# A spectral layer and a mixture of experts on one core: biases moved from TensorE to VectorE, the inverse spread over the steps

## The chip, the cores and the metric

The kernel runs on one core of a Trainium2 chip. The metric is the device time of the program in microseconds (us). TensorE is PE in the profile, its weight loads PEld, VectorE DVE, ScalarE ACT, GpSimd POOL, and SyncE, which issues most transfers, SP.

## The reference

```python
X = np.fft.rfft(x, axis=1)                 # x: 8 x 2496 x 256
Yr = Xr @ w_r - Xi @ w_i + b_r
Yi = Xr @ w_i + Xi @ w_r + b_i
Yr = np.sign(Yr) * np.maximum(np.abs(Yr) - 0.01, 0.0)      # Yi the same
y = np.fft.irfft(Yr + 1j * Yi, n=2496, axis=1)
# mixture of experts over the 19968 rows of y, 8 experts, the best one each:
out[mask] = gate_w[mask] * (np.maximum(y[mask] @ w1[e], 0) @ w2[e])
```

## The kernel before

The transform of length 2496 = 39 x 64 is done as two matrix products with a trip through DRAM between them. `fwd_a` (L280) does the 39-point part for two groups of a batch: a product pa into a PSUM bank of the tag "u", copied to ae and written to the spectrum in DRAM; eleven of them make a batch. `turn` (L295) reads the spectrum back transposed, as t. A **step** is one of ten slices of a batch, 80 in all, and step it = 10 b + s is slice s of batch b.

In a step, `fwd_b` (L302) does the 64-point part of the next step's slice as pb, and `halves` (L313) splits it into a rounded part sh and a rest sl, because the products with the weights are done as three products of rounded halves: ACT reads pb into re and sh, DVE makes the sum su and sl, then ACT and DVE make the third slot of sh and sl from su. `mix` (L328) multiplies: pk is the product with w_r of the sum, copied by ACT to k; pm holds the two others, and DVE adds k to both, giving the tile v (u in the code). The biases are added on PE: each half of pm begins with a product of a tile of ones and a tile that holds the bias in two rows (L335, `split_bias`, L252). `shrink` (L355) is the soft threshold of the step before: ACT makes r, DVE four pieces of y. `inv_b` (L371) multiplies y of an earlier step back to 64 points (pv, tag "u"), and ACT copies it into z, which holds a whole batch.

`inv_a` (L384) is the last part: of twelve **pieces** of a batch, each does two groups of pz from z (tag "u", one product that also gives the gate's logits), split by ACT and DVE into zh and zl, and the py of the piece before (tag "yo"), copied by ACT to yb. z has one copy, so the pieces of batch b-1 are all done in steps 2 to 5 of batch b, three a step ("turning"), and the pv of those steps wait till step 6, two a step, held as y in six buffers.

After eleven groups `route` (L581) is queued as a job: 23 small DVE operations, an exponential (ex, L594) on ACT and two small products, cut into pieces that `tick` emits one by one. They give each token its expert, its gate and its slot; `scatter` writes the rows to the experts' lists in DRAM by indirect transfers on POOL, `send` one by one, held back by `pace`. `table` gives the experts' tiles of 256 tokens. The last batch's pieces are interleaved with the first seven tiles (`finish_last`, L551), and 82 tiles are done in all (`up`, L885, and `down`, L914).

The order of every engine but POOL is the order of the code. PSUM has eight banks: four of tag "u" (pa, pv, pz, and po of the first tiles), two of "yo" (py, pk and the routing's), one for pb, one for pm.

Of the kernel before, what the change touches and what calls it, by code (L numbers as in the profile page):

```python
# [100 lines left out]
class Kernel:  # L101
    def __init__(self, tc, nb, x, w_r, w_i, b_r, b_i, w_gate, w1, w2,
# [6 lines left out]
        assert (nb - 3) * S - E * (TT - 1) > (EARLY - 1) * TT  # L109
# [27 lines left out]
    def open_inverse(self, st, pst):  # L137
# [35 lines left out]
        self.z = k.tile([128, 2, 66, 40], F32, name="z")  # L173

    def open_forward(self, st):
# [3 lines left out]
        self.xp = self.pool(self.xst, "xp", 5)  # L179
# [9 lines left out]
        self.bias = f.tile([128, 2, D], F32R, name="bias")  # L189
        self.ones = f.tile([128, 128], F32R, name="ones")  # L190
# [6 lines left out]
        self.braw = self.w.tile([33, 2, D], F32, tag="y", name="braw", bufs=6)  # L197
        for h, b in ((0, self.b_r), (1, self.b_i)):
            for q in (0, 32):
                nc.gpsimd.dma_start(self.braw[q:q + 1, h, :], b.rearrange("(o n) -> o n", o=1))  # L200
# [11 lines left out]
        nc.gpsimd.memset(self.z[:, :, 64:66, :], 0.0)  # L212
# [39 lines left out]
    def split_bias(self):  # L252
        nc = self.nc
        zero = self.w.tile([128, 2, D], F32, tag="y", name="zero", bufs=6)
        nc.vector.memset(zero, 0.0)
        nc.vector.tensor_copy(self.bias, zero)
        nc.vector.tensor_scalar_add(self.ones, zero[:, 0, 0:128], 1.0)
        bh = self.w.tile([33, 2, D], F32R, tag="y", name="bh", bufs=6)
        nc.scalar.copy(self.bias[0:1], self.braw[0:1])
        nc.scalar.copy(bh[32:33], self.braw[32:33])  # L260
        nc.vector.tensor_sub(self.bias[32:33], self.braw[32:33], bh[32:33])

# [65 lines left out]
    def mix(self, b, s):  # L328
# [3 lines left out]
        def product(nm, slot, to):  # L332
            i = 0 if nm == "r" else 1
            if i:
                nc.tensor.matmul(to, self.ones, self.bias[:, 1 if nm == "d" else 0, :], start=True, stop=False)  # L335
            for c in range(2):
                for a, ww in ((sh, self.wh), (sh, self.wl), (sl, self.wh)):
                    nc.tensor.matmul(to, a[:, c, slot, :], ww[nm][:, c, :], start=i == 0, stop=i == (5 if nm == "r" else 6))
# [13 lines left out]
        nc.vector.tensor_add(u, p, k.unsqueeze(1).broadcast_to((128, 2, D)))  # L352
        self.us[b, s] = u

    def shrink(self, b, s):  # L355
# [5 lines left out]
        y = self.w.tile([128, 2, D], F32, tag="y", name="y", bufs=6)  # L361
# [9 lines left out]
    def inv_b(self, b, s):  # L371
        nc = self.nc
        y = self.ys.pop((b, s))
        p = self.psi.tile([128, 512], F32, tag="u", name="pv", bufs=4).rearrange(
            "p (c a r n) -> p c a r n", c=2, a=2, r=2)
        for kp in range(2):
            for c in range(2):
                nc.tensor.matmul(p[:, c, kp, :, :], y[:, kp, c * 128:(c + 1) * 128], self.bi[:, 2 * s + kp, :],  # L378
                                 start=True, stop=True)
        for c in range(2):  # L380
            nc.scalar.copy(self.z[:, c, 0:NB, 4 * s:4 * s + 4].rearrange("p n a -> p a n"),  # L381
                           p[:, c].rearrange("p a r n -> p (a r) n"))

    def inv_a(self, b, i):  # L384
        nc = self.nc
        for g in (2 * i, 2 * i + 1) if i < GH else ():
            p = self.psi.tile([128, 512], F32, tag="u", name="pz", bufs=4)
            for c in range(2):
                nc.tensor.matmul(p[:120, c * 136:(c + 1) * 136],  # L389
                                 self.z[:, c, 3 * g:3 * g + 3, :].rearrange("p j a -> p (j a)"), self.iw[:, c, :],  # L390
# [6 lines left out]
        for g in (2 * i - 2, 2 * i - 1) if i else ():  # L397
# [10 lines left out]
    def spectral(self, fwd):  # L408
# [14 lines left out]
        self.split_bias()  # L423
        self.turn(0, 0)
        self.turn(0, 1)
# [28 lines left out]
        for it in range(n):  # L454
# [16 lines left out]
            if turning:  # L471
                inverse()
# [538 lines left out]
```

## Time and profile before

| | |
|---|---|
| median of 3 runs | 1549.95 us (1549.72 to 1550.38) |
| the profiled execution: time, span | 1556.04 us, 1554.3 us |
| mean granted TensorE clock | 0.992 of full speed |
| DVE, ACT, POOL busy | 59%, 50%, 25% of the span |
| HBM read, written | 241.99 MB, 66.37 MB |

The spectral part runs to about 582 us, and the rest is the last batch's pieces and the tiles. A timeline row gives start, duration and the instruction, with the number of instructions merged in the row; a duration reaches to the end of the last write, so the next instruction of an engine may start before it. The length of a repeated step is therefore read from start to start.

### The profile page before, as it was taken

The numbers are of one execution on the slowest core, as the hardware profiler recorded it, in microseconds if no ns is written. First come the engines' busy times: TensorE is split into PE (matmuls) and PEld (weight loads), VectorE is DVE, ScalarE is ACT, GpSimd is POOL, SyncE is SP. The second block draws the span as 40 slices with busy tenths as digits, with TensorE's granted clock in tenths as the row PEclk, the third lists the DMA queues.
The fourth block names the chain that finished last, engine by engine and source line by source line (L and its number), as shares of the span: only waits on it lengthen the run. The fifth ranks groups of instructions, "written<-read, shape, count | busy, mean of one in ns | idle before, by whom it ended". The sixth has DMA issues, their size and how long they took to land. (4 is left out here: it accounts for less than half of the span.)

```text
span 1554.3 us, 35598 instructions
## 1 busy us (share of the span) xinstructions
PE 1516.7 (98%) x10934; PEld 1398.6 (90%) x10934; DVE 912.2 (59%) x2102; ACT 782.2 (50%) x1689; POOL 394.8 (25%) x554
## 2 busy tenths in 40 slices
PE   6999999999999999999999999999999999999997
PEld 3899999998989888889999999999999999999996
DVE  3677787777778777655455545545445445445442
ACT  2667777777767666344344434434334334334332
POOL 1002433425151534334311111111112111111111
PEclk7999999999999999999999999999999999999998
DMA  8864554646353422334234332323213213132210
GB/s 238 231 193 115 174 145 136 179 119 195 111 172 94 147 58 61 84 91 121 65 100 106 95 77 72 97 52 94 56 42 98 49 47 103 42 78 69 49 42 21
DMA packets 192834, 159.94 MB, mean 103 GB/s; under 512 B 127770, under 2 KB 163264, under 8 KB 192365
## 3 DMA queue, kind: packets, MB, share of 16 engines
q1 hardware_dynamic: 172685, 113.43, 28.8%
q0 software_dynamic: 19936, 44.04, 8.5%
q8 instruction: 89, 1.46, 0.4%
q14 instruction: 124, 1.02, 0.2%
HBM read 241.99 MB, written 66.37 MB: 198 GB/s over the span
## 5 line engine op out<-in xcount | busy, mean ns | idle before, releaser
L939 PE MATMUL po<-h,hh 128*128 128x512 f32 x1312 | 462.1, 395 | 0.0
L902 PE MATMUL ph<-xh,h 128*128 128x256 f32 x1312 | 372.0, 284 | 1.8 <-DVE hl L908 1.8
L902 PE MATMUL ph<-xl,h 128*128 128x256 f32 x1312 | 371.1, 283 | 0.0
L902 PE MATMUL ph<-xh,l 128*128 128x256 f32 x1312 | 370.7, 283 | 0.0
L936 PE MATMUL po<-h,hl 128*128 128x256 f32 x1148 | 324.0, 282 | 0.2 <-DVE hl L908 0.2
L908 DVE SCALAR_TENSOR_TENSOR hl<-ph,hh 128x512 fp32r<-128x512 f32 x328 | 226.2, 690 | 149.3 <-ACT hh L907 114.2
L907 ACT ACTIVATE hh<-ph 128x512 fp32r<-128x512 f32 x328 | 193.8, 597 | 204.0 <-PE ph L902 198.4
L939 PEld LDWEIGHTS po<-h,hh 128*128 128x128 f32 x1312 | 241.5, 188 | 43.8 <-issue 0.2
L948 POOL DMA_INDIRECT out<-o,row x124 | 123.8, 998 | 581.1 <-DVE o L946 472.7
L902 PEld LDWEIGHTS ph<-xh,l 128*128 128x128 f32 x1312 | 251.0, 191 | 3.7
L902 PEld LDWEIGHTS ph<-xh,h 128*128 128x128 f32 x1312 | 251.0, 191 | 3.2 <-DVE hl L908 3.2
L946 DVE SCALAR_TENSOR_TENSOR o<-po,xr,part 128x256 f32<-128x256 f32 x156 | 75.4, 484 | 302.6 <-ACTq L864 153.7
L902 PEld LDWEIGHTS ph<-xl,h 128*128 128x128 f32 x1312 | 251.1, 191 | 0.0
L945 ACT ACTIVATE part<-po,xr 128x256 f32<-128x256 f32 x156 | 73.8, 473 | 334.1 <-PE po L939 324.9
L936 PEld LDWEIGHTS po<-h,hl 128*128 128x128 f32 x1148 | 215.6, 188 | 6.3 <-DVE hl L908 2.1
L644 POOL DMA_INDIRECT xs_dram<-yb,pos x176 | 176.7, 1004 | 74.4 <-issue 63.8
L365 DVE SCALAR_TENSOR_TENSOR y<-v,r 64x256 f32<-64x256 f32 x320 | 134.0, 419 | 6.9 <-ACT r L359 0.8
L389 PE MATMUL pz<-iw,z 128*120 128x136 f32 x704 | 96.9, 280 | 2.5 <-DVE zl L395 1.7
L308 PE MATMUL pb<-bm,t 128*128 128x128 f32 x640 | 86.8, 279 | 12.3 <-DMA t<-spec_dram 9.5
L381 ACT COPY z<-pv 128x256 f32<-128x256 f32 x160 | 94.3, 712 | 5.9 <-PE pv L378 2.9
L308 PEld LDWEIGHTS pb<-bm,t 128*128 128x128 f32 x640 | 80.0, 195 | 13.5 <-issue 11.2
L389 PEld LDWEIGHTS pz<-iw,z 128*120 128x120 f32 x704 | 87.7, 183 | 3.5 <-DVE zl L395 1.9
(181 smaller groups left out, 2557.7 us busy)
## 6 DMA issues: line engine op xcount, KB each, us to landing
r<-moe_w SPq DMA_DIRECT2D x672, 128.0 KB
r<-moe_w SPq DMA_DIRECT2D x166, 512.0 KB
xq<-xs_dram SPq DMA_DIRECT2D x332, 64.0 KB
spec_dram<-ae SPq DMA_DIRECT2D x88, 240.0 KB
t<-spec_dram SPq DMA_DIRECT2D x160, 128.0 KB
x<-x SPq DMA_DIRECT2D x40, 384.0 KB
x<-x SPq DMA_DIRECT2D x40, 84.0 KB
xs_dram<-yb,pos POOLq DMA_INDIRECT x176
```

The costliest lines, as they stand in the source:

```text
L308: nc.tensor.matmul(p[:, c, :, kp, :], t[:, kp, c * 128:(c + 1) * 128], self.bm[:, 2 * s + kp, :], start=True, stop=True)
L365: nc.vector.scalar_tensor_tensor(out=y[q * 64:q * 64 + 64, kp, :], in0=u[h, q, :], scalar=LAM, in1=r[h, q, :], op0=ALU.add, op1=ALU.min)
L381: nc.scalar.copy(self.z[:, c, 0:NB, 4 * s:4 * s + 4].rearrange("p n a -> p a n"), p[:, c].rearrange("p a r n -> p (a r) n"))
L389: nc.tensor.matmul(p[:120, c * 136:(c + 1) * 136], self.z[:, c, 3 * g:3 * g + 3, :].rearrange("p j a -> p (j a)"), self.iw[:, c, :], start ...
L644: i = nc.gpsimd.indirect_dma_start(out=self.xs[:, :], out_offset=bass.IndirectOffsetOnAxis(ap=pos[:n, g:g + 1], axis=0), in_=y[:n, g, 0:XW ...
L902: nc.tensor.matmul(p[:, i, :], a[:, c, f * 128:(f + 1) * 128], v[:, c, :], start=m == 0, stop=m == 5)
L907: nc.scalar.activation(hh[:, s, :], p, AF.Relu)
L908: nc.vector.scalar_tensor_tensor(out=hl[:, s, :], in0=p, scalar=0.0, in1=hh[:, s, :], op0=ALU.max, op1=ALU.subtract)
L936: nc.tensor.matmul(p[:, :D], hl[:, f - 1, hs], w2[:, f - 1, 0, :], start=False, stop=False)
L939: nc.tensor.matmul(p, hh[:, f, hs], w2[:, f].rearrange("p a d -> p (a d)"), start=f == 0, stop=f == 7)
L946: nc.vector.scalar_tensor_tensor(out=o[:, h, :], in0=p[:, :D], scalar=xr[:, h, 0:1], in1=part, op0=ALU.mult, op1=ALU.add)
L948: i = nc.gpsimd.indirect_dma_start(out=self.out[:, :], out_offset=bass.IndirectOffsetOnAxis(ap=at[h], axis=0), in_=o[:, h, :], in_offset=N ...
```

## The change

z gets a second copy, used by even and odd batches in turn. The twelve pieces of a batch are spread over steps 2 to 11 behind the batch's own ten, one or two a step, and each pv is done two steps behind its mix. The two bias matmuls of each step go: the biases are loaded to all partitions by two transfers (the old row tiles, tile of ones and `split_bias` go), and k becomes a DVE operation that adds both biases to pk and writes twice the width. pk gets a bank of its own, and tag "u" has three banks. The first routing pieces of a step stand between v and su. The last two pieces of batch 6 stand behind the last step, where eight filler products stood. There are four x tiles in place of five, five ae in place of eight, three y in place of six; the first table is made from step 56 on in place of 61, and a step sends two or three scattered groups of rows in place of three.

```diff
-        assert (nb - 3) * S - E * (TT - 1) > (EARLY - 1) * TT
+        assert (nb - 4) * S - E * (TT - 1) > (EARLY - 1) * TT
...
-        self.z = k.tile([128, 2, 66, 40], F32, name="z")
+        self.zs = [k.tile([128, 2, 66, 40], F32, name=f"z{i}") for i in range(2)]
...
-        self.xp = self.pool(self.xst, "xp", 5)
+        self.xp = self.pool(self.xst, "xp", 4)
...
-        self.bias = f.tile([128, 2, D], F32R, name="bias")
-        self.ones = f.tile([128, 128], F32R, name="ones")
+        self.bias = f.tile([128, 2, D], F32, name="bias")
...
-        p = self.psi.tile([128, 512], F32, tag="u", name="pa", bufs=4)
+        p = self.psi.tile([128, 512], F32, tag="u", name="pa", bufs=3)
...
-        ae = self.xp.tile([120, 2, D], F32, tag="ae", name="ae", bufs=8)
+        ae = self.xp.tile([120, 2, D], F32, tag="ae", name="ae", bufs=5)
...
         def product(nm, slot, to):
-            i = 0 if nm == "r" else 1
-            if i:
-                nc.tensor.matmul(to, self.ones, self.bias[:, 1 if nm == "d" else 0, :], start=True, stop=False)
+            i = 0
...
-        pk = self.psi.tile([128, 512], F32, tag="yo", name="pk")
+        pk = self.psi.tile([128, 512], F32, tag="k", name="pk", bufs=1)
         product("r", 2, pk[:, :D])
-        k = self.w.tile([128, D], F32, tag="k", name="k", bufs=2)
-        nc.scalar.copy(k, pk[:, :D])
-        self.pace(k[0:1, 0:1])
+        k = self.w.tile([128, 2, D], F32, tag="k", name="k", bufs=2)
+        nc.vector.tensor_add(k, pk[:, :D].unsqueeze(1).broadcast_to((128, 2, D)), self.bias)
+        self.pace(k[0:1, 0, 0:1])
...
-        nc.vector.tensor_add(u, p, k.unsqueeze(1).broadcast_to((128, 2, D)))
+        nc.vector.tensor_add(u, p, k)
...
-        y = self.w.tile([128, 2, D], F32, tag="y", name="y", bufs=6)
+        y = self.w.tile([128, 2, D], F32, tag="y", name="y", bufs=3)
...
     def inv_a(self, b, i):
+        self.inv_z(b, i)
+        self.inv_y(b, i - 1)
...
-        self.split_bias()
         self.turn(0, 0)
         self.turn(0, 1)
+        for h, v in ((0, self.b_r), (1, self.b_i)):
+            self.nc.sync.dma_start(self.bias[:, h, :], bass.AP(v.tensor, v.offset, [[0, 128], [1, D]]))
...
         for b in range(nb):
             for s in range(10):
-                o = s + 2 if b == 0 or s > 7 else 6 + s // 2
-                if 10 * b + o < n:
-                    back[10 * b + o].append((b, s))
+                if 10 * b + s + 2 < n:
+                    back[10 * b + s + 2] = (b, s)
+        pieces = {i: [] for i in range(n)}
+        for b in range(nb - 1):
+            for i, o in enumerate((2, 3, 3, 4, 5, 5, 6, 7, 8) if b == nb - 2 else (2, 3, 4, 4, 5, 6, 7, 8, 8, 9, 10, 11)):
+                pieces[10 * b + 10 + o].append((b, i))
...
+            self.tick(3 if it < n - 10 else 4)
             if it + 1 < n:
                 self.fwd_b(*todo[it + 1])
                 half = self.halves(*todo[it + 1])
                 next(half)
...
             mix = self.mix(b, s)
+            next(mix)
+            for _ in itertools.chain(small, half):
+                pass
...
             for a in first[it]:
                 self.fwd_a(*a)
+            if back[it]:
+                for _ in self.inv_b(*back[it]):
+                    pass
             self.tick(1)
+            self.nudge()
+            for a in pieces[it][:1]:
+                self.inv_a(*a)
             next(mix, None)
+            self.tick(3 if it >= n - 5 else 1)
+            self.nudge()
+            if s % 2 or b >= nb - 2:
+                self.pace(self.us[b, s][0:1, 0, 0:1])
+                self.send(1)
+            for a in pieces[it][1:]:
+                self.inv_a(*a)
...
-            if b == nb - 2 and s == 1:
+            if b == nb - 3 and s == 6:
                 self.tabling = self.table(0)
...
-        self.keep_warm(8)
-        self.inv_b(*todo[n - 1])
+        self.inv_z(nb - 2, 9)
+        self.inv_y(nb - 2, 8)
+        self.inv_z(nb - 2, 10)
+        self.tick(3)
+        for _ in self.inv_b(*todo[n - 1]):
+            pass
+        self.inv_y(nb - 2, 9)
+        self.inv_y(nb - 2, 10)
...
     def breathe(self):
-        self.tick(3)
-        self.nudge()
+        self.tick(4)
...
-                self.psi.tile([128, 512], F32, tag="u", name="po", bufs=4)
+                self.psi.tile([128, 512], F32, tag="k" if h else "u", name="po", bufs=1 if h else 3)
```

The places where the order matters, as the engines' programs have it (a row is a line of the kernel, the instruction, what it writes and reads; xN: so many alike).

PE, from the last product of pk on; before, in a step with two pv:

```order
L338 MATMUL pk<-whr,sl 128x256
L284 MATMUL pa<-x,far 120x512
L378 MATMUL pv<-bi,y 128x128 x4
L335 MATMUL pm<-bias,ones 128x256
L338 MATMUL pm<-whd,sh 128x256
L338 MATMUL pm<-wld,sh 128x256
```

The same place of the change, in a step with one piece:

```order
L321 MATMUL pk<-whr,sl 128x256
L269 MATMUL pa<-x,far 120x512
L361 MATMUL pv<-bi,y 128x128 x4
L377 MATMUL pz<-iw,z_107 120x136 x4
L394 MATMUL py<-zh,gh 117x272
L394 MATMUL py<-zh,gl 117x272
L394 MATMUL py<-zl,gh 117x272
```

The bias product is gone, pv stands behind pa, and pz and py of a piece stand between them and pm.

ACT, a step with an exponential of a routing job; before:

```order
L319 COPY re<-pb 128x256
L320 CAST sh<-pb 128x2x256
L359 ACTIVATE r<-v,nlam 128x512
L324 CAST sh<-su 128x2x128
L594 ACTIVATE ex<-lg 117x88
L381 COPY z<-pv 128x4x64 x2
L344 COPY k<-pk 128x256
L292 COPY ae<-pa 120x512
```

and of the change, from the eviction of py on:

```order
L395 COPY yb<-py 117x272 x2
L585 ACTIVATE ex<-lg 117x88
L304 COPY re<-pb 128x256
L305 CAST sh<-pb 128x2x256
L342 ACTIVATE r<-v,nlam 128x512
L309 CAST sh<-su 128x2x128
L277 COPY ae<-pa 120x512
L365 COPY z_108<-pv 128x4x64 x2
```

ex stood behind re, sh, r and sh, and stands ahead of them now.

DVE, around su, with the last operations of a routing job; before:

```order
L352 TENSOR_TENSOR v<-pm,k 128x512
L321 TENSOR_TENSOR su<-re,pb 128x256
L322 TENSOR_TENSOR sl<-pb,sh 128x2x256
L325 TENSOR_TENSOR sl<-su,sh 128x2x128
L626 TENSOR_TENSOR carry<-carry,scan_102 117x8
L628 CAST carry_b<-carry 117x8
L630 SCALAR_TENSOR_TENSOR rb<-pr,base 117x8
L365 SCALAR_TENSOR_TENSOR y<-v,r 64x256 x2
L633 TENSOR_TENSOR lg<-scan_102,rb 117x88
```

and of the change:

```order
L335 TENSOR_TENSOR v<-pm,k 128x512
L617 TENSOR_TENSOR carry<-carry,scan_102 117x8
L619 CAST carry_b<-carry 117x8
L621 SCALAR_TENSOR_TENSOR rb<-pr,base 117x8
L624 TENSOR_TENSOR lg<-scan_102,rb 117x88
L625 TENSOR_TENSOR lg<-lg,scan_100 117x88
L306 TENSOR_TENSOR su<-re,pb 128x256
L307 TENSOR_TENSOR sl<-pb,sh 128x2x256
L327 TENSOR_TENSOR k<-pk,bias 128x512
L348 SCALAR_TENSOR_TENSOR y<-v,r 64x256 x4
```

The five routing operations stood behind su and sl and among the pieces of y, and stand between v and su now; the new k stands between sl and y.

## Rows read from the trace of the kernel before

**Rows 1.** The page of the profiled execution: its span, and busy time by engine.
```profile
span 1554.3 us, 35598 instructions
...
PE 1516.7 (98%) x10934; PEld 1398.6 (90%) x10934; DVE 912.2 (59%) x2102; ACT 782.2 (50%) x1689; POOL 394.8 (25%) x554
```

**Rows 2.** Stretches A:B in us: length, busy time by engine (instructions), clock, DMA share, GB/s.
```profile
99.81:450.39 350.58, 349.79 (x2703) 322.41 (x2702) 265.67 (x740) 258.41 (x635) 125.40 (x209) 1.00 0.51 147
450.39:494.42 44.03, 41.89 (x326) 38.79 (x324) 33.75 (x116) 29.89 (x79) 10.02 (x16) 1.00 0.34 99
494.42:576.74 82.32, 78.93 (x652) 76.05 (x651) 66.89 (x191) 56.38 (x139) 35.25 (x57) 1.00 0.41 113
```

**Rows 3.** PE in order of time, step 9 (start us, us, instruction).
```profile
78.87 1.05 PE L308 MATMUL pb<-bm,t 128*128 128x128 f32 x8
79.76 1.06 PE L378 MATMUL pv<-bi,y 128*128 128x128 f32 x8
80.58 0.36 PE L338 MATMUL pk<-whr,sh 128*128 128x256 f32 x1
...
81.38 1.02 PE L284 MATMUL pa<-x,far 117*120 117x512 f32 x2
...
83.07 0.28 PE L335 MATMUL pm<-bias,ones 128*128 128x256 f32 x1
83.18 0.28 PE L338 MATMUL pm<-whs,sh 128*128 128x256 f32 x1
...
83.89 0.61 PE L308 MATMUL pb<-bm,t 128*128 128x128 f32 x4
```

**Rows 4.** PE in order of time, one inverse piece in a turning step.
```profile
243.25 1.09 PE L389 MATMUL pz<-iw,z 128*120 128x136 f32 x8
244.09 0.37 PE L403 MATMUL py<-zh,gh 120*117 120x272 f32 x1
...
244.92 0.28 PE L335 MATMUL pm<-bias,ones 128*128 128x256 f32 x1
```

**Rows 5.** DVE in order of time, the same step 9.
```profile
79.14 0.69 DVE L352 TENSOR_TENSOR v<-pm,k 128x512 f32<-128x512 f32 x1 [0.25 <-PE pm L338]
80.91 0.42 DVE L321 TENSOR_TENSOR su<-re,pb 128x256 f32<-128x256 f32 x1 [1.08 <-ACT sh L320]
81.25 0.68 DVE L322 TENSOR_TENSOR sl<-pb,sh 128x512 fp32r<-128x512 f32 x1
81.85 0.42 DVE L325 TENSOR_TENSOR sl<-su,sh 128x256 fp32r<-128x256 f32 x1
82.18 1.73 DVE L365 SCALAR_TENSOR_TENSOR y<-v,r 64x256 f32<-64x256 f32 x4
```

**Rows 6.** ACT in order of time, the same step 9.
```profile
80.02 0.37 ACT L319 COPY re<-pb 128x256 f32<-128x256 f32 x1 [1.49 <-PE pb L308]
...
81.68 1.17 ACT L381 COPY z<-pv 128x256 f32<-128x256 f32 x2
...
82.96 0.59 ACT L292 COPY ae<-pa 120x512 f32<-120x512 f32 x1
```

**Rows 7.** Groups by line, 99.81 to 450.39 us: count, busy, mean ns, idle before, releasers.
```profile
L395 DVE TENSOR_TENSOR zl<-pz,zh 120x272 fp32r<-120x272 f32 x110 | 44.1, 434 | 3.4 <-ACT zh L394 1.9 <-issue 0.4
...
L344 ACT COPY k<-pk 128x256 f32<-128x256 f32 x50 | 21.3, 425 | 1.2 <-PE pa L284 0.8 <-PE pz L389 0.5
L321 DVE TENSOR_TENSOR su<-re,pb 128x256 f32<-128x256 f32 x50 | 21.1, 421 | 51.9 <-PE pz L389 23.0 <-ACT sh L320 16.0 <-ACT re L319 5.2
```

**Rows 8.** DVE in order of time, two operations of a routing job.
```profile
261.87 0.24 DVE L587 TENSOR_TENSOR lg<-yb 117x88 f32<-117x88 f32 x1
262.15 0.24 DVE L590 TENSOR_REDUCE mx<-lg 117x11 f32<-117x88 f32 x1
```

**Rows 9.** PE in order of time, behind the last step.
```profile
576.74 1.49 PE L378 MATMUL pv<-bi,y 128*128 128x128 f32 x8
...
582.25 0.99 PE L389 MATMUL pz<-iw,z 128*120 128x136 f32 x4 [0.74 <-ACT z L381]
```

More of the change, by code (lines that the diff above doesn't have):

```diff
@@ L211, in open_forward @@
         nc.gpsimd.dma_start(self.tcol, self.c_tcol)
-        nc.gpsimd.memset(self.z[:, :, 64:66, :], 0.0)
+        for z in self.zs:
+            nc.gpsimd.memset(z[:, :, 64:66, :], 0.0)
     def load_w(self, nm):
@@ L250, in split_weights @@
         split("s")
[L252 to L261, printed above, removed]
     def split_inverse(self):
@@ L396, in inv_a, with inv_y @@
             self.hl[g] = h, l
-        for g in (2 * i - 2, 2 * i - 1) if i else ():
+    def inv_y(self, b, i):
+        nc = self.nc
+        for g in (2 * i, 2 * i + 1) if i >= 0 else ():
             if g % GH == 0:
@@ L461, in spectral @@
                 next(half)
-            turns = iter(range(3 * s - 6, 3 * s - 3) if turning else ())
-            def inverse():
-                if back[it]:
-                    self.inv_b(*back[it].pop(0))
-                for i in turns:
-                    self.inv_a(b - 1, i)
-                    break
-            if turning:
-                inverse()
             if it:
@@ L475, in spectral @@
                 next(small)
-            next(half, None)
-            self.tick(2)
-            self.nudge(it)
-            if not turning:
-                inverse()
-            mix = self.mix(b, s)
-            if not turning:
-                next(mix)
-            for a in first[it]:
-                self.fwd_a(*a)
-            if turning:
-                next(mix)
-            next(small, None)
-            self.tick(2)
-            self.nudge(it)
-            inverse()
-            next(small, None)
+            mix = self.mix(b, s)
+            next(mix)
+            for _ in itertools.chain(small, half):
+                pass
             if it:
@@ L495, in spectral @@
                 self.send(1)
+            for a in first[it]:
+                self.fwd_a(*a)
+            if back[it]:
+                for _ in self.inv_b(*back[it]):
+                    pass
             self.tick(1)
+            self.nudge()
+            for a in pieces[it][:1]:
+                self.inv_a(*a)
             next(mix, None)
-            inverse()
-            self.tick(1)
-            self.pace(self.us[b, s][0:1, 0, 0:1])
-            self.send(1)
+            self.tick(3 if it >= n - 5 else 1)
[5 more added lines that the diff above has]
+                self.inv_a(*a)
             for a in loads[it]:
@@ L540, in send, with nudge @@
                 n -= 1
-    def nudge(self, it=0):
-        for _ in range(2 if it % 10 < 7 else 0):
-            if next(self.tabling, "wait") == "wait":
-                break
+    def nudge(self):
+        next(self.tabling, None)
     def breathe(self):
-        self.tick(3)
-        self.nudge()
+        self.tick(4)
     def finish_last(self):
@@ L620, in route @@
         nc.vector.tensor_copy(sb, pa[:, GH - 1, :])
-        for _ in range(8 if b >= self.nb - 3 else 4):
+        for _ in range(8):
             yield
```

35 lines of the change are left out of this document (19 added, 16 removed).

## Prediction

> **What bounds the kernel now.** The profiled execution spans 1554.3 us and TensorE (PE) is busy in 98% of it [rows 1]; its whole time is 1556.0 us, 6.1 us above the median of the three runs, 1549.95 us. My sum is a difference within the profiled execution, and I take it off the median. 0.2% of that, 3.1 us, is about what a measurement of this kernel can tell from no change.
>
> The second view cuts the spectral part into stretches. From 99.81 to 450.39 us (steps 12 to 61, five whole batches) PE is busy 349.79 of 350.58 us at clock 1.00: what PE executes there is the time, and a matmul taken away is time gained. From 450.39 to 494.42 (steps 62 to 66) it loses 2.1 us, from 494.42 to 576.74 (steps 67 to 79) 3.4, and the 5.51 us from 576.74 to the first pz of the last batch at 582.25 hold eight filler matmuls [rows 2, 9]. VectorE (DVE) is busy 265.67 of 350.58 us, 76% [rows 2], but not free to choose when: every step it sits idle about 1.04 us before su (51.9 us over 50 steps) [rows 7]. Step 9 shows why: v starts 0.27 us behind the start of pb, su only 2.04 us behind it, when ACT has read the same bank [rows 3, 5].
>
> **The change, part by part.**
>
> *The bias matmuls.* 160 go. In step 9 one stands at 83.07, the next matmul at 83.18, and six in a row take 0.71 us, so 0.118 us each [rows 3]. That is 0.236 us a step and 18.9 us in all, the full price wherever PE is the bound.
>
> *The add on DVE, the copy off ACT.* The nearest row to the new k is sl, also a two-input operation of 128x512 out of PSUM: 0.68 us, and the next one starts 0.60 us behind it [rows 5]. 80 adds are 48 us. ACT loses 80 copies of 0.425 us [rows 7]; it was busy 258 of 351 us [rows 2], so that is worth nothing by itself. Bounds of the add on the path: nothing (DVE waits anyway) and 0.60 us a step. The Trainium skill ("Advanced Engine Details and Errata", TRN2 Errata) speaks against this move: ScalarE is the engine closer to PSUM, VectorE the one closer to SBUF. The Trainium skill's "Perfetto Trace Analysis" (Optimizing Scalar/DVE Operations) puts the access at some 125 ns on VectorE and 51 on ScalarE; by its figures, an estimate, each move would cost 0.07 us more than it frees, 6 us over 80 steps if all of it were on the path, and my forecast would rise by as much. The sum itself goes by sl, whose 0.60 us has the PSUM access in it.
>
> *Does DVE still fit behind PE?* A batch takes PE 350.58/5 - 10 x 0.236 = 67.8 us. DVE is busy 53.1 us a batch; with ten adds 59.1. With the idle 10.4 us before su it would be 69.5 and too long. But the change puts the routing steps just there, behind v: the order shows 5 to 9 of them between a v and the next su. A routing job has 23 small operations; a dependent pair is 0.28 us apart and one lasts 0.24 [rows 8], others read one after another are shorter, and I take 4.9 us a job (23 x 0.28 = 6.4 is the upper end). Two jobs a batch, most of it in the gap: some 63 of 67.8 us. So PE stays the bound in the steady part, with little room.
>
> *Stalls of the new order.* PE needs 0.89 us for pb, 0.82 for pv, 0.80 for pk and 0.86 for pa (1.69 from pa to the second bias, less seven slots of 0.118) [rows 3], and 0.42 for a group of pz [rows 4]; the new order is pb, pk, pa, pv, pz, pz. Read from the start of pb: pk from 0.89, pa from 1.69, pv from 2.55, the first pz at 3.37, the second at 3.79. With three banks in place of four the second pz takes the bank of this step's pa, so ACT must have written ae by 3.79. ACT starts re 1.15 behind pb, is through sh, r and sh at 2.81, and ae takes 0.59: 3.40 [rows 3, 6]. That leaves 0.39 us. Once per routing job ex now stands on ACT ahead of re, and waits for three operations behind v: v ends for the next at 0.87, plus three times 0.28, plus ex about 0.24 like the operations of its shape [rows 5, 8]: re starts at 1.95, 0.80 late, and the second pz waits 0.4. Ten jobs in steps 12 to 61: 4.0 us. What is late next is y and with it nothing: pv reads a y two steps old. Bounds: nothing, and a wait in every step (rival 3).
>
> *The spread inverse and second z.* A piece is 1.67 us of PE wherever it stands (pz 0.84, py 0.83) [rows 4]. Its moving changes no total, only which steps are long.
>
> *Steps 62 to 66.* Ordinary steps are 5.02 us [rows 3], without bias 4.78; with six pz and five py pairs 33.1 us, and one late ex: 33.5.
>
> *Steps 67 to 79.* No pa is left, so PE is short: 13 x (0.89 + 0.80 + 0.82 + 12 x 0.118) less one pb, and 14 pieces of 1.67: 73.5 us. DVE: su 0.34, sl 0.60, k 0.60, y 1.73, sl 0.33, v 0.60 are 4.2 us [rows 5], 13 times less 1.3 for the last step; 28 zl at some 0.40 (mean 0.434, overlapping) [rows 7]; three jobs of 4.9: together 79.2. Taking the longer engine step by step gives about 81, and three late ex add 0.8 each: 83.5. Here DVE is the bound and the adds count whole.
>
> *Behind the last step.* The fillers go; two groups of batch 6 stand in their place. The chain v, r, y, pv, z, pz is what it was, 5.51 us [rows 9]; with the extra pz and py I take 6.0.
>
> From 450.39 to the first pz of the last batch: 33.5 + 83.5 + 6.0 = 123.0 against 44.03 + 82.32 + 5.51 = 131.9: 8.9 us less.
>
> *Edits at nothing.* Four x buffers, five ae and the biases fetched behind the second turn: the start moves the same bytes and its first pb waits for the spectrum, not for them; 0 to 2 us, I take 0.5. split_bias ran while that transfer was awaited: 0. Three y instead of six: a y lives two steps: 0. Last pieces: po shares three banks with pz, one wait of about the time of an ACT and a DVE operation: 1 us. The new positions of the table and the scattered rows run on POOL and in DVE's gaps: 0, and if the rows fell behind, yb copies on ACT would be late next.
>
> **Sum.** Steps 0 to 11: -12 x 0.236 = -2.8. Steps 12 to 61: -11.8 + 4.0 = -7.8. The end of the spectral part: -8.9. Start and last pieces: +1.5. Together -18.0, so 1549.95 - 18 = **1532 us**.
>
> **The rivals.**
>
> 1. *PE is fed throughout.* No late ex and DVE never decides: -2.8 - 11.8, and the end at PE's own 33.1 + 73.5 + 6.0 = 112.6 instead of 131.9: -34, 1516 us. For it: 349.79 of 350.58. Against it: DVE's 79 us against PE's 73.5 at the end.
>
> 2. *The add lies on the path in every step* (the slower side). Place: DVE between sl and y in steps 12 to 61. Price: 50 x (0.60 - 0.236) = +18.2, with the rest at -10.2: +8, 1558 us. It decides from the point where 0.236 + 10.2/50 = 0.44 of the 0.60 us is on the path. For it: 59.1 + 10.4 us a batch if the gap before su stays. Against: the routing steps moved into that gap.
>
> 3. *The pa bank is late in ordinary steps too.* If su is late by 0.3 us beyond its margin of 0.39 in each of some 55 steps, the second pz waits 16 us in all: -2, about no change, 1548 us. For it: three banks; against: ACT loses a copy per step.
>
> 4. *The clock.* A step with its PE matmuls at 1.2 GHz instead of 2.4 would be longer by its own 6.45 us; twelve such steps behind the stalls are +77: 1609 us. In stretches where PE lost 2.1 and 3.4 us the granted clock stayed 1.00 [rows 2], so I give it little. The Trainium skill ("TensorE: Matmul & The Clock Gate", A second HAM failure mode) tells of a kernel that cycled PSUM banks and whose clock swung from the short idle times; by that rule this case would come, and the trace does not agree so far.
>
> **How the numbers follow.** Forecast 0.64, with a range of its own of 1524 to 1541 (ex stalls from nothing to twice mine, the end 4 us either way); rival 1 0.12; rival 2 0.11; rival 3 0.10; rival 4 0.03. Range 1516 to 1553: it leaves out rival 4, the upper two thirds of rival 2 and the tip of rival 1. Faster: 0.64 + 0.12 + 0.04 of rival 3 = 0.80. Same: 0.05 of rival 3. Slower: rivals 2 and 4 and 0.01 of rival 3 = 0.15.
>
> **What would show it.** Right: no bias rows; steady batches of 67 to 69 us with PE busy nearly throughout; DVE busy about 87% there; small waits of pz for ae, at most one per job; in steps 67 to 79 DVE busy over 90% and PE waiting for sl or v. Wrong: pz or pk waiting in ordinary steps, batches of 70 us or more (rivals 2 and 3), a granted clock below 1.00 after 100 us (rival 4), or the last 13 steps below 78 us (rival 1). The prediction is wrong in its core if the bias matmuls go and the steady batch is not shorter by at least 1 us.

## The result, and the profile after

The changed kernel takes 1564.10 us (median of 4 runs, 1562.54 to 1566.49) against 1549.84 us before in the same session: ratio 1.0094, interval 1.0077 to 1.0112. It is slower by some 14 us, where 18 us less were forecast. Its profiled execution took 1562.54 us. Its page, and stretches of its windows: the first three are cut where [rows 2] are cut, the fourth runs from step 67 to the last batch's first pz:

```profile
span 1560.8 us, 35422 instructions
PE 1499.3 (96%) x10766; PEld 1377.8 (88%) x10766; DVE 962.1 (62%) x2186; ACT 757.6 (49%) x1615; POOL 392.2 (25%) x551
```

```profile
core 0: us, PE busy (x) PEld busy (x) DVE busy (x) ACT busy (x) POOL busy (x), PEclk, DMA share, GB/s
100.27:450.81 350.54, 341.41 (x2601) 310.91 (x2600) 293.25 (x785) 238.74 (x584) 108.51 (x180) 1.00 0.51 145
450.81:487.07 36.26, 34.06 (x262) 31.05 (x261) 32.02 (x102) 23.66 (x58) 16.57 (x29) 1.00 0.40 117
487.07:572.97 85.90, 77.88 (x647) 75.03 (x645) 76.22 (x212) 53.29 (x134) 37.88 (x65) 1.00 0.40 113
487.07:581.60 94.53, 84.93 (x697) 81.22 (x695) 80.98 (x222) 58.66 (x148) 42.62 (x72) 1.00 0.38 107
```

Against [rows 1], PE is busy 98% before and 96% now: it does less, and stands still more. Steps 12 to 61 last 350.54 us as before (350.58), but PE is busy 341.41 of them instead of 349.79: the matmuls went, the time stayed. PE's waits in that stretch (engine, line, releaser: us, times, longest):

```profile
PE pz L377 <- ACT ae L277: 8.0, 12, 1.2
PE py L394 <- ACT yb L395: 0.6, 1, 0.6
```

By the prediction's own test it is wrong in its core: the bias matmuls went, and a steady batch takes 70.11 us on average, as before (70.12).

Here it is in one step, number 33. First DVE, from v on; then ACT; then PE (start, length, engine, line; in brackets the idle time before and who ended it):

```profile
245.98 0.68 DVE L335 TENSOR_TENSOR v<-pm,k 128x512 f32<-128x512 f32 x1
246.58 0.24 DVE L596 TENSOR_TENSOR scan<-lg,mx 117x88 f32<-117x88 f32 x1
...
247.36 1.04 DVE L605 TENSOR_TENSOR scan<-scan 117x88 f32<-117x88 f32 x4
248.43 0.17 DVE L611 CAST sb<-scan 117x8 bf16<-117x8 f32 x1
248.51 0.42 DVE L306 TENSOR_TENSOR su<-re,pb 128x256 f32<-128x256 f32 x1
```

```profile
246.11 0.59 ACT L305 CAST sh<-pb 128x512 fp32r<-128x512 f32 x1
246.70 0.72 ACT L342 ACTIVATE r<-v,nlam 128x512 f32<-128x512 f32 x1
248.96 0.40 ACT L309 CAST sh<-su 128x256 fp32r<-128x256 f32 x1 [1.54 <-DVE su L306]
249.28 0.58 ACT L277 COPY ae<-pa 120x512 f32<-120x512 f32 x1
```

```profile
244.69 1.05 PE L293 MATMUL pb<-bm,t 128*128 128x128 f32 x8
...
248.05 0.63 PE L377 MATMUL pz<-iw,z 128*120 128x136 f32 x4
249.91 0.72 PE L377 MATMUL pz<-iw,z 128*120 128x136 f32 x4 [1.24 <-ACT ae L277]
```

Routing fills DVE from v to su, so su starts 3.82 us behind pb (2.04 in [rows 3, 5]). The second half of sh waits 1.54 us for it, ae stands behind that on ACT although pa was long done, and the second pz needs pa's bank. One step earlier in a job, at s = 2, ex does the same from the other end (ACT in step 22, and PE's wait there):

```profile
169.86 0.28 ACT L585 ACTIVATE ex<-lg 117x88 f32<-117x88 f32 x1 [2.21 <-DVE lg L582]
170.04 0.35 ACT L304 COPY re<-pb 128x256 f32<-128x256 f32 x1
170.29 0.59 ACT L305 CAST sh<-pb 128x512 fp32r<-128x512 f32 x1
...
171.69 0.60 ACT L277 COPY ae<-pa 120x512 f32<-120x512 f32 x1
```

```profile
172.34 0.72 PE L377 MATMUL pz<-iw,z 128*120 128x136 f32 x4 [0.42 <-ACT ae L277]
```

PE had pb at 167.93; re could have run from about 169.1 (1.15 behind pb, [rows 6]) and ran at 170.04. The Trainium skill ("PSUM — Partial Sum Buffer", Engine vs sequencer instructions) calls ScalarE's queue strictly first in, first out; the rows agree: re, sh and ae start behind ex, one after the other.

### The profile page after: what moved, and what is told of

It is laid out like the page before. It is cut to its first block, busy times and chain, and to the rows that moved or that the text cites. A ratio compares the mean times of both kernels' runs of the same rounds, so it can differ in the third digit from the quotient of the medians.

```text
span 1560.8 us, 35422 instructions
## 1 busy us (share of the span) xinstructions
PE 1499.3 (96%) x10766; PEld 1377.8 (88%) x10766; DVE 962.1 (62%) x2186; ACT 757.6 (49%) x1615; POOL 392.2 (25%) x551
## 5 line engine op out<-in xcount | busy, mean ns | idle before, releaser
L635 POOL DMA_INDIRECT xs_dram<-yb,pos x176 | 180.0, 1023 | 93.7 <-issue 53.6
L377 PE MATMUL pz<-iw,z 128*120 128x136 f32 x704 | 101.7, 283 | 17.8 <-ACT ae L277 10.1
L361 PEld LDWEIGHTS pv<-bi,y 128*128 128x128 f32 x640 | 82.9, 191 | 33.4 <-issue 25.8
```

Source lines behind the costliest of these rows:

```text
L377: nc.tensor.matmul(p[:120, c * 136:(c + 1) * 136], self.zs[b % 2][:, c, 3 * g:3 * g + 3, :].rearrange("p j a -> p (j a)"), self.iw[:, c, : ...
L635: i = nc.gpsimd.indirect_dma_start(out=self.xs[:, :], out_offset=bass.IndirectOffsetOnAxis(ap=pos[:n, g:g + 1], axis=0), in_=y[:n, g, 0:XW ...
```

## The experiments

The kernel before took 1556.2 us beside e1 to e8, and 1549.3 to 1549.6 us beside e9 to e17. Chips 6 and 14 are on record at both levels, so the chip alone does not explain them; their cause is open. Ratios are therefore compared within a level, and stages by their traces. "Finish" is the stretch from the first pz of the last batch to the first ph of the seventh tile.

**e12 and e13, the two kernels once more.** No edit.

> The changed kernel as it is, on the chip of the other experiments, where the kernel before takes 1556.2 us instead of 1549.9. Between the two profiled executions there were only 6.5 us, between the medians 14.3. If the profiled execution of the kernel before was slow by itself, the ratio here is 1.009 again, some 1570 us; if the kernel before has times that depend on the chip and the changed one less so, 1.003-1.006.

> The kernel before as it is, once more with a profile. Its profiled execution that the prediction was worked from took 1556.04 us, 6.1 above the median beside it. If that execution had a slow start (the start waits for transfers: step 2 of the changed kernel began at 47.37 us in one profile and 49.95 in another), steps 12 to 61 take 350.6 us again and the difference lies before step 12. If it was another stage (the expert part behind 690 us, which no experiment touches), steps 12 to 79 are as before and the difference lies behind. An execution of 1556 us here too would say that the time depends on the chip.

e12: 1563.18 us, ratio 1.0089 [1.0073, 1.0104]; steps 12 to 61 take 350.56 us. So the changed kernel repeats beside a kernel before of 1549.6 us. It was not run beside one of 1556.2, so whether it is slower there too is not shown. e13: 1549.68 us, span 1547.9. Against the execution that the prediction was worked from, step 12 starts 0.7 us earlier, steps 12 to 61 take 1.2 us less, and from step 62 to the last batch's first pz it takes 126.60 us instead of 131.86 (step 62: 8.49 for 10.85, steps 72 and 73 together 16.30 for 18.89); the rest is equal within a microsecond. Why those steps were slow in the first profile stays open; its execution, 1556.04 us, was at the level of e1 to e8. For the result, beside 1549.84 us, e13 is the fair measure, and by it the miss falls out like this (us):

| stage | before (e13) | changed | forecast difference | measured |
|---|---|---|---|---|
| start to step 12 | 99.10 | 100.27 | -2.3 | +1.2 |
| steps 12 to 61 | 349.34 | 350.54 | -7.8 | +1.2 |
| step 62 to first pz of the last batch | 126.60 | 130.79 | -8.9 | +4.2 |
| finish | 96.46 | 102.75 | +1.0 | +6.3 |
| rest | 876.40 | 876.45 | 0 | 0 |

Together +12.9 us, as the executions have it (1562.54 - 1549.68).

**e1: the fourth bank back.**

```diff
-tag="u", name="pa", bufs=3     (pv, pz, pw alike; po from "k" and "u")
+tag="u", name="pa", bufs=4     (po from "u" alone)
-pk = self.psi.tile([128, 512], F32, tag="k", name="pk", bufs=1)
+pk = self.psi.tile([128, 512], F32, tag="yo", name="pk")
```

> The changed kernel with four u banks again: pk goes back to the two yo banks that it shared with py, and po takes its banks from u alone; nothing else differs. Theory A (the third bank): in steps 12 to 61 the second pz waits for ae because it takes the bank of this step's pa (10 us of waits of pz for ae over 14 places in the changed kernel). With four banks it takes an older one, so these waits go, the batches fall from 70.4-71.5 to 68-69 us and the whole from 1564 to 1551-1556 us. Theory B (VectorE is the bound): the adds and the routing steps fill VectorE in the short steps, the bank is only where it shows; the wait moves to pk for sl or to py for zl, batches stay at 70 us or more and the time within 3 us of 1564.

1565.51 us, 1.0065 [1.0047, 1.0082]; steps 12 to 61 take 351.14 us. No wait of pz for ae is left, and the time is not shorter: py now waits for k, 5.6 us in 4 times, since pk lies in py's banks. So this exchange gains nothing: the fourth bank of "u" is the one that pk had for itself. What a fourth bank alone would do is not shown.

**e2: ae ahead of the second sh.**

```diff
+            for a in first[it]:
+                self.fwd_a(*a)
             for _ in itertools.chain(small, half):
                 pass
...
-            for a in first[it]:
-                self.fwd_a(*a)
```

> The changed kernel with pa's copy ae ahead of the second half of sh on ScalarE instead of behind it (the call moves up by one place; on TensorE pa stays behind pk, three u banks stay). Theory A, in the form that ae is late because it stands behind sh, which waits for su on VectorE: ae then comes 0.6 us behind pa whatever VectorE does, the pz waits for ae fall from 10 us to under 2, batches to 68-69 us, the whole to 1551-1556 us. Theory B (VectorE is the bound): no difference, 1561-1567 us, the wait moves to another matmul.

1559.81 us, 1.0024 [1.0013, 1.0035]; steps 12 to 61 take 346.52 us, 4.0 less, and pz waits 0.6 us for ae. All batches but the first still take 69.1 us and more. Of the 11.7 us that the stretch had over PE's own 338.8, a third was ae's place.

**e3 and e4: the bias alone, in the old and out of the new order.** e3 is the kernel before without the bias matmuls, with the biases fetched as in the change and k added on DVE; e4 is the changed kernel with the bias matmuls and the copy k of the kernel before (edits shortened).

```diff
e3: -i = 0 if nm == "r" else 1
    -if i: nc.tensor.matmul(to, self.ones, self.bias[...], start=True, stop=False)
    +i = 0
    -nc.scalar.copy(k, pk[:, :D])
    +nc.vector.tensor_add(k, pk[:, :D].unsqueeze(1).broadcast_to((128, 2, D)), self.bias)
e4: the same lines the other way, in the changed kernel
```

> The kernel before with only the bias moved: no bias matmuls, the biases fetched behind the second turn, k as one add of 128x512 on VectorE, everything else (four u banks, old order, one z, bunched inverse) as before. The bias part by itself, by the prediction's term: 160 matmuls of 0.118 us are 18.9 us; with the adds hidden in VectorE's idle time before su the time falls to 1531-1538 us. If the adds lie on the path (rival 2 of the prediction) they cost up to 0.60 us a step for 0.236 gained: 1550-1575 us.

> The changed kernel with the bias back on TensorE: two bias matmuls a step, k copied on ScalarE, split biases as in the kernel before; three u banks, the new order and the spread inverse stay. Theory A: TensorE has 0.236 us a step more to do, which in the short steps only shortens the waits for ae; 1562-1572 us, and pz still waits for ae behind the first steps of a batch. Theory B (the adds on VectorE are what costs): without the adds VectorE has 48 us less to do, the waits go and the time is at or below the kernel before, 1545-1552 us.

| steps 12 to 61, us | bias on PE | bias on DVE |
|---|---|---|
| old order | 350.58 (349.34 in e13) | 354.00 (e3) |
| new order | 360.55 (e4) | 350.54 |

e3: 1565.76 us, 1.0064 [1.0044, 1.0083]. In the old order the add gives nothing: ordinary steps gain their 0.236 us, but those with s = 2, 4, 5 and 8 grow by 0.2 to 0.5, so that the first four batches last 279.96 us for 279.75; the fifth is an exception with 74.04: re begins up to 4.7 us behind pb in its steps 59 and 60, and the granted clock falls to 0.83 there; the cause is open. That is the mechanism of rival 2, in four steps of ten and not in every one. e4: 1572.53 us, 1.0111 [1.0091, 1.0132]. In the new order the bias part is worth 10.0 us in this stretch, and the order with the bias on PE costs 10.0 by itself. So the adds are not what costs; the order is. The two do not simply add: with the adds on DVE, the order gains 3.5 us (354.00 to 350.54).

**e8: the old order with routing behind v.**

```diff
+            self.tick(2)          (ahead of fwd_b)
...
             next(half, None)
-            self.tick(2)
```

> On the kernel before with the bias on VectorE (e3, ratio 1.0064): two of the five routing steps move from behind the second half of sl to the top of the step, between v and su. In e3 the ordinary steps gained their 0.236 us, and the steps with the bunched inverse (s = 2 to 5) and s = 8 lost 0.5 to 0.8 us each, which gave it back. If the adds are on the path only because the gap before su stands empty (the prediction's reason why the sum could count the adds as hidden), the batches fall from 70.0 to 68-69 us, ratio 0.998-1.002. If the steps with the inverse are full on VectorE or the routing makes su late: batches 70-71 us, ratio 1.005 or more.

1557.90 us, 1.0012 [1.0001, 1.0023]; the first three batches take 68.5 to 69.2 us where e3 takes 69.8 to 70.1. Routing in the gap before su does hide part of the add, as the prediction's sum assumed.

**e5 and e6, both on e2: fewer routing steps behind v; ex behind sh.**

```diff
e5: -self.tick(3 if it < n - 10 else 4)      +self.tick(1 if it < n - 10 else 4)
    -self.tick(1)   (behind pv)              +self.tick(3 if it < n - 10 else 1)
e6: -self.tick(3 if it < n - 10 else 4)   (ahead of fwd_b)
         nc.scalar.copy(sh[:, :, 0:2, :], v)
    +    yield
                 next(half)
    +            self.tick(3 if it < n - 10 else 4)
    +            next(half, None)
```

> On the kernel with ae first (e2, ratio 1.0024): of the three routing steps that stand at the top of a step, between v and su, two move behind y and the second half of sl (1 at the top, 3 behind pv, 1 behind v; 5 a step as before), up to step 69. In e2 a batch takes 69.1-69.6 us against 67.8 us of TensorE work, and the loss lies in three steps per batch: about +0.5 where a job's exponential falls (s = 8 and 2) and +0.9 at s = 4. Theory C (the routing steps between v and su make su late in the steps in which a job runs): the losses shrink, batches 68.0-68.6 us, 4 to 7 us less than e2, ratio 0.998-1.000. Theory B (VectorE is simply full in those steps, wherever the routing stands): batches stay at 69.1-69.6 us and the ratio at 1.001-1.004.

> On the kernel with ae first (e2, ratio 1.0024): the three routing steps at the top of a step are put behind re and sh in the program, still ahead of su: VectorE's order is the same, and on ScalarE the exponential ex stands behind sh instead of ahead of re; the small matmul of a job comes behind pb. Theory D (ex is the stall of the prediction, 0.4 us once per job): re and sh are on time in those steps, and the ten steps with an ex in steps 12 to 61 are some 0.5 us shorter, 4 to 6 us in all: batches 68.2-68.6 us, ratio 0.999-1.000. Theory C (it is the routing on VectorE, not ex): under 1.5 us gained, ratio 1.001-1.003.

e5: 1569.78 us, 1.0091 [1.0072, 1.0110], steps 12 to 61 take 354.28 us: worse by 7.8 than e2, with py waiting 11.9 us for yb up to 700 us. Theory C in this form falls: routing taken out of the gap costs more here than it gives back. e6: 1551.87 us, 0.9977 [0.9964, 0.9991], 341.43 us. DVE's order is as in e2; ex moves on ACT, and a small product of the job on PE, and that is worth 5.1 us.

**e9: ex behind sh alone,** on the changed kernel (e6's edit without e2's).

> The changed kernel with only the place of ex changed (as in e6), ae still behind the second half of sh. e6 has both edits and its five batches take 341.4 us against 350.5 of the changed kernel and 346.5 of e2. Theory D (one cause: ex ahead of re on ScalarE holds re, sh, the second sh and ae; moving ae helped only because ae stood at the end of that row): 341-344 us for steps 12 to 61, ratio 0.998-1.001, nearly no wait of pz for ae. Theory A+D (two causes that add: ex, and su late on VectorE holding the second sh and with it ae): only the 5 us of e6 over e2 go, 345-346 us, ratio 1.003-1.006, and the waits of pz for ae at s = 3, where no ex falls, stay.

1558.01 us, 1.0061 [1.0045, 1.0076]; steps 12 to 61 take 344.52 us, and PE's waits there are:

```profile
PE pz L378 <- ACT ae L277: 5.0, 4, 1.3
PE py L395 <- ACT yb L396: 0.6, 1, 0.6
```

Of 12 waits for ae the 4 of the steps without ex are left. The causes add: 350.56 (e12), 344.52 without ex's wait, 338.92 with ae moved too (e10, same group): 6.0 + 5.6 us. The steps agree: against e9, e10 is shorter by 1.5 us at s = 3 and longer by 0.2 at s = 4. e6, at the other level, has the same two edits and takes 341.43; in it re begins up to 0.8 us late in 13 of these steps, in e10 in one. Why is open, as is what that level costs e2 and e6.

**e7 and e10: start and end.** e7 stands on e2, e10 on e6. Both bring the biases as one row; e7 leaves no inverse piece behind the loop, e10 routes more slowly in the finish.

```diff
-self.nc.sync.dma_start(self.bias[:, h, :], bass.AP(v.tensor, v.offset, [[0, 128], [1, D]]))
+nc.gpsimd.dma_start(self.brow[:, h, :], b.rearrange("(o n) -> o n", o=1))
+self.nc.tensor.matmul(p, self.one, self.brow.rearrange("p h d -> p (h d)"), start=True, stop=True)
+self.nc.vector.tensor_copy(self.bias.rearrange("p h d -> p (h d)"), p)
e7:  -(2, 3, 3, 4, 5, 5, 6, 7, 8) if b == nb - 2   (and inv_z, inv_y of that batch behind the loop)
     +(2, 2, 3, 3, 4, 4, 5, 6, 6, 7, 8, 8) if b == nb - 2
e10: -self.breathe()   (in the loop over pieces: 4 steps)      +self.tick(2)
```

> On the kernel with ae first (e2), two stages changed that do not touch steps 12 to 61. Start: the biases come as one row (2 KB) on the POOL queue and are spread over 128 partitions by one matmul with a row of ones, instead of a fetch of 256 KB on SP's queue behind the second turn. Theory E (that fetch delays the turns: step 2 starts at 45.37 us in the kernel before, 45.72 in e4, which has no such fetch, but 47.37 to 48.6 us in the four kernels that have it): step 2 starts at 45.3-46.0 us, 2 to 2.5 us gained. If the spread matmul or another transfer is the cause: no gain. End: the last inverse pieces of the seventh batch go back into its steps 70 to 78 (as in the kernel before, where no piece was left behind the loop), instead of behind the last step. Theory F (the job of its second half, routed behind the loop, is what makes the stretch from the first pz of the last batch to the eighth tile 7 us longer): that stretch falls from 114.5 to 108-110 us, and the steps 67 to 79 grow by at most 5. Rival: VectorE is full in both stretches, what is gained in the one is lost in the other, no net gain at the end.

> The kernel of e6 (ratio 0.9977) with two further stages changed. Start: the biases as one row and one matmul (as in e7, where step 12 began at 96.66 instead of 101.53 us): step 12 begins at 96-97 us, 4 us gained. Finish: during the last inverse pieces 2 routing steps per piece instead of 4, 4 per part of a tile as before: if the jobs of two half batches among VectorE's zl, l and h there are the cause of the longer finish (the trace of the changed kernel shows pz waiting 5 us for zl between 581 and 600 us, and VectorE without a gap from 583.65 us), the second tile begins 2 to 4 us earlier behind the first pz of the last batch than in e6 (37.8 us, in the kernel before 33.2). If the work is only pushed into the next tiles, the seventh tile begins as late as in e6 (102.8 us). Whole: 0.992-0.996 by the first, 0.995-0.997 by the second.

e7: 1558.35 us, 1.0015 [1.0005, 1.0024]. PE's pb of step 2, first in the changed kernel, then in e7:

```profile
47.37 1.13 PE L293 MATMUL pb<-bm,t 128*128 128x128 f32 x8 [1.63 <-DMA t<-spec_dram]
```

```profile
44.32 1.05 PE L298 MATMUL pb<-bm,t 128*128 128x128 f32 x8
```

With the fetch on SP's queue step 2 starts at 47.4 to 50.0 us in nine profiles, without it at 44.3 to 45.7 in ten: theory E holds. e7's end is 4.1 us longer than e2's and its finish 1.6 shorter, but its clock fell around the border of the two (below). e10: 1545.76 us, 0.9975 [0.9966, 0.9985], faster than both kernels. Its steps 12 to 61:

```profile
97.41:436.33 338.92, 338.28 (x2601) 310.55 (x2600) 291.65 (x786) 242.86 (x584) 108.06 (x180) 1.00 0.53 150
```

PE is busy all of it, at the 338.8 us that the prediction gave for PE alone. The finish is 3.9 us shorter than in e6, and the rest 3.0 longer (879.36): pushed on rather than gained.

**e11: e10 with the last 13 biases on TensorE** (edit shortened).

```diff
+late = 10 * b + s >= 10 * self.nb - 13
+if late and nm != "r": nc.tensor.matmul(to, self.one, self.bias[0:1, h, :], start=True, stop=False)
+k: nc.scalar.copy if late, else nc.vector.tensor_add
```

> e10 with the last 13 steps (67 to 79, without pa) in the manner of the kernel before: k copied on ScalarE and the biases added on TensorE (by a matmul of one row), so VectorE loses 13 adds of 0.6 us and TensorE gains 26 small matmuls. If VectorE is the bound there (the prediction's term for steps 67 to 79, which counts the adds whole), the stretch from step 67 to the first pz of the last batch falls from 94.4 us by 4 to 8 us. If the stretch is set by the chains between the engines and not by VectorE's sum, it stays within 2 us or grows.

1564.35 us, 1.0105 [1.0090, 1.0121]: from step 67 to the first pz 110.42 us, 14.5 more. It does not test what it was to test, because the one-row matmuls in f32 cost 0.82 us each. But ordinary steps there grew by just that, 1.64 for two, from 5.59 to 7.23: they hang on PE, not on DVE. e4 says more: with no adds on DVE it takes 73.47 us for steps 67 to 77, the changed kernel 73.35, though e4's PE has 11 x 0.236 = 2.6 us more to do. So the adds cost there some 2.5 of their 6.6 us, an estimate from these sums.

**e14: one piece later; e15 to e17: the finish.** e14 is e10 with the doubled pieces one step on. e15 and e17 are e14 with no piece left behind the loop and 3 routing steps per piece, spread or bunched; e16 is e14 with 4 routing steps per piece.

```diff
e14: -(2, 3, 3, 4, 5, 5, 6, 7, 8)    +(2, 3, 4, 4, 5, 6, 6, 7, 8)
e15: +(2, 2, 3, 3, 4, 4, 5, 5, 6, 6, 7, 7)    e17: +(2, 2, 3, 3, 3, 4, 4, 4, 5, 5, 5, 6)
e16: -self.tick(2)    +self.tick(4)
```

> e10 (ratio 0.9975) with one edit in the last steps: the doubled inverse pieces of the seventh batch move from steps 73 and 75 to steps 74 and 76. In e10 step 73 takes 11.30 us with 7.3 us of TensorE work (two pieces of 1.67 and 3.93 of the step), and in the changed kernel VectorE has no gap there from 523.36 to 535 us, with a routing job, four zl and the adds in it. If VectorE is full in that step because two pieces and the routing job fall together, the doubled piece one step later, when the job is past, shortens steps 72 to 77 by 2 to 4 us (from 42.94 in e10) and the ratio is 0.995-0.997. If VectorE is full over several steps, the loss moves along with the pieces: within 1 us, ratio 0.997-0.998.

> e14 (ratio 0.9961) with the twelve inverse pieces of the seventh batch in steps 72 to 77, two in each, none behind the loop, and 3 routing steps per piece in the finish instead of 2 (as in the kernel before). By theory F the finish is longer because the routing job of the seventh batch's second half runs there: with the job nearly done when the loop ends, the seventh tile begins 96 to 98 us behind the first pz of the last batch (96.46 in e13, 98.91 in e14) and what stands behind it is 876.4 us again (879.2 in e14); the stretch from step 62 to that pz, 127.16 in e14, may grow by up to 3. Ratio 0.993-0.996. If the finish is long for another reason: 101 us or more, ratio 0.998 or more.

> e14 with 4 routing steps per piece in the finish again, as the change has it. e10's 2 steps per piece brought the seventh tile 3.9 us forward, but what stands behind it grew by 3.0 us (879.36 against 876.37): if the routing is VectorE work that is only moved, e16 takes 102.8 and 876.4 us for the two and its whole time is 0.9 us above e14's, ratio 0.996-0.998. If e14's slow routing is a real gain, e16 is 3 us or more above it, ratio 0.998-1.000.

> e15 with the twelve pieces of the seventh batch bunched into steps 72 to 76 (2, 3, 3, 3, 1), close to the kernel before, so that the job of the second half is done before the loop ends. The finish is then that of the kernel before if the job is its whole excess: 96 to 97 us (theory F). The full steps 73 to 75 cost more: by the prediction's VectorE sum of 4.2 us a step, 0.8 us for a piece's two zl and 5 routing steps of 0.21 to 0.28, a step with three pieces takes VectorE about 7.9 us against 8.9 of TensorE, so TensorE stays ahead by a little and the stretch from step 62 is within 2 us of e15's. If VectorE decides there, it is 3 us or more longer.

| | us | ratio | step 62 to pz | finish | rest |
|---|---|---|---|---|---|
| e14 | 1544.22 | 0.9961 [0.9947, 0.9976] | 127.16 | 98.91 | 879.21 |
| e15 | 1547.64 | 0.9986 [0.9976, 0.9995] | 133.49 | 99.94 | 876.35 |
| e16 | 1544.61 | 0.9968 [0.9957, 0.9980] | 127.17 | 102.85 | 876.52 |
| e17 | 1548.04 | 0.9994 [0.9985, 1.0004] | 134.81 | 99.13 | 876.45 |

e14: steps 72 to 77 take 41.02 instead of 43.23 us (the 42.94 of the expectation is not e10's time for them), 2.2 of the 2 to 4 expected; step 74 is the long one now (9.96). The loss moved along in part. e16: the slow routing was only a shift; its 0.4 us are within the noise. e15 and e17: without the leftover job the finish is 2.9 and 3.7 us shorter than e16's, and its second tile begins 33.95 and 33.20 us behind that pz, as before the change (33.2, 34.4). Their routing is slower too, 3 steps per piece for 4; but that alone only shifted time to the rest (e16 against e14), and here the rest is no longer. So the job is probably that part of the finish; e7, where only its place changed, gained 1.6 us there, with the clock at 0.50 to 0.89 in the first 8. The remaining 3 us or so are open, and in e15 the clock (below) has a share in them. The stretch ahead grew by 6.3 and 7.6 us, and no version gains from it. e14 has the lowest time, 0.4% below the kernel before; e16 is not told apart from it.

## Why the prediction was wrong

- **The bias matmuls:** right. In the order that leaves PE fed, steps 12 to 61 take 338.92 us (e10); forecast without stalls, 338.8.
- **The add on DVE:** nearly right in the new order: with it the bias part gains 10.0 (e4 to the changed kernel) of the 11.8 us; the first batch, without a job in its first steps, took 67.66 us (67.8 forecast), and with the bias on PE the order loses nearly as much (10.0 against 11.7 us). In the old order it gained nothing.
- **The stall by late ex:** this step failed. 0.4 us, once per job, 4.0 us in all, "what is late next is y and with it nothing". ex costs 6.0 us (e9), and what the prediction left out 5.6 (e10): in the next steps of the job the routing makes su late, the second sh waits for su on ACT, and ae waits behind that sh. The margin of 0.39 us was worked out for ae with su on time, 2.04 us behind pb; with the routing behind v it came at 3.82. Rival 3 named this chain and put it at 16 us, but spread it thinly over all steps.
- **Steps 62 to 66:** 36.26 for 33.5 us, by the same two waits; without them 34.1 (e6, e10).
- **Steps 67 to 79:** the first pv behind the last step begins at 572.97 us, 85.9 behind step 67, for 83.5. "Here DVE is the bound and the adds count whole" failed as put: DVE is busy 76.22 of these 85.90 us, 89%, but steps 69, 70, 76 and 77, with one piece, take 5.59 to 5.67 us, PE's own 3.93 + 1.67 (e11). The loss lies in the steps with two pieces, 8.57 us (68) and 11.09 (73) for 7.27, and in those beside 73, some 0.8 (72) and 1.2 us (74). Step 67, 6.65 us, holds eight matmuls of the first table (pq, some 1.0 us), which the sum left out. In step 73 DVE does decide:

```profile
526.20 0.38 PE L321 MATMUL pk<-whr,sl 128*128 128x256 f32 x1 [1.04 <-DVE sl L310]
533.28 0.72 PE L377 MATMUL pz<-iw,z 128*120 128x136 f32 x4 [1.42 <-DVE zl L383]
```

- **Behind the last step:** 8.63 for 6.0 us: the pieces there wait for zl and yb, and four groups of py stand between the last pv and the first pz.
- **The start, 0.5 us:** "the same bytes" left out the fetch of 256 KB, which delays the turns: step 12 is 2.8 us late (100.27 for 97.5), and one row in its place regains 4.9 (e2 to e7) and 3.6 (e6 to e10).
- **The last pieces, 1 us:** 6.3. The sum has three routing jobs in steps 67 to 79, and three run there; a fourth, of batch 6's second half, it has nowhere. It runs here, from 582 to 597 us, and pz waits for zl 0.99, 2.84 and 1.16 us between 584 and 592. About half of the 6.3 us probably goes with it (e15, e17), the other half is open.
- **The measure:** 5.3 us of the end's -8.9 were slow steps of one profiled execution.
- **Rival 1** is what e10 shows in the steady part. **Rival 4** did not come: the granted clock is 1.00 in every window of 5 us from 60 to 700 us. In e12 two windows, 590 to 600 us, have 0.74 and 0.92, and its finish is 0.3 us longer.

## What to carry to other kernels

Where an engine takes its work in order, an instruction that waits for another engine holds all that stands behind it, also the copy that frees a PSUM bank: when work is moved ahead of such a wait, list everything behind it, not only the instruction that comes next in the data flow. Here a gain on the bounding engine was lost where the next engine's chain had no margin, in the fullest steps, so work the margin out there and not for the average. And a stage that was slow in one profile is no stage to count on: look at a second profile before its time goes into a sum.

## What the runs showed of the hardware

The clock that rival 4 was about did fall in some of these runs. In e15 neither the fillers of the kernel before nor the pieces of the changed one stand on PE behind the last step (windows of 5 us):

```profile
560.00:565.00 5.00, 3.10 (x25) 2.69 (x23) 4.66 (x15) 1.34 (x3) 2.53 (x5) 1.00 0.11 33
565.00:570.00 5.00, 2.52 (x13) 2.18 (x10) 3.02 (x11) 2.86 (x5) 4.18 (x7) 0.55 0.30 90
570.00:575.00 5.00, 5.00 (x23) 4.98 (x23) 2.48 (x5) 2.43 (x8) 1.66 (x3) 0.50 0.17 51
575.00:580.00 5.00, 4.77 (x35) 4.38 (x35) 4.62 (x11) 5.00 (x16) 2.69 (x4) 0.93 0.11 36
```

PE was busy 3.10 and 2.52 of 5 us, the granted clock went from 1.00 (2.4 GHz) to 0.50 (1.2 GHz), and the matmuls behind took twice as long: eight pv 2.05 us instead of 1.05. e7 and e17, also with neither, show the same (0.50). But e8, which has the fillers, falls to 0.50 too, at 595 us in the finish, behind a window in which PE was busy 2.75 of 5 us. Smaller falls stand in e1, e2, e3 and e10 to e14 (0.66 to 0.97), and e12 among them is the changed kernel. None stands between 60 and 700 us in the first profiles of the two kernels, nor in e4, e5, e6, e9 and e16. So neither the fillers nor the pieces kept the clock up in every run, and what either does for it is not shown. The Trainium skill ("TensorE: Matmul & The Clock Gate", A second HAM failure mode) tells of a kernel whose clock swung from short idle times between groups of matmuls that cycled through PSUM banks. The trace of the changed kernel does not agree: the 12 waits of its steps 12 to 61, up to 1.24 us each, left the clock at 1.00.

A matmul of one row of contraction is not cheap in f32: the two biases of a step in e11 lengthened it by 1.64 us, 0.82 each, where the kernel before paid 0.118 each [rows 3] with tiles of 128 rows in fp32r.
